# Decode attention with a GLU beside it: more filler matmuls near the end, one copy on one engine, one product in another PSUM bank

## The chip, the cores and the metric

One core of a Trainium2 chip runs the kernel. The metric is the device time of one launch in microseconds. "TensorE" does the matmuls (PE in the profile, its weight loads PEld), "VectorE" is DVE, "ScalarE" ACT, "GpSimd" POOL, and "SyncE" (SP) issues the DMAs.

## The reference

One decode step of a parallel block for two sequences (B = 2), everything in float32: a layer norm, then attention over the last 2048 positions of a cache with 32 heads of 128, and beside it a bilinear GLU.

```python
W = min(4096, max(256, Sk // 4))                      # 2048 of 8192 positions
q = (xn @ wq).reshape(B, 1, 32, 128)                  # xn = layernorm(x), D = 512
scores = einsum("bhqd,bhkd->bhqk", q, k_cache[:, :, Sk - W:]) * 128 ** -0.5
o = einsum("bhqk,bhkd->bhqd", softmax(scores), v_cache[:, :, Sk - W:])
out = x + o.reshape(B, 1, 4096) @ wo + ((xn @ w_gate) * (xn @ w_up)) @ w_down   # F = 1376
```

## The kernel before

The caches and all weights, some 159 MB, are laid out beforehand as one stream in the order of their use, and SyncE loads it piece by piece into three `step` buffers of 54 KB a partition. `blocks` writes that order out by hand; `pump` issues the next piece when all fields of an old one have been used (`done`). At the end of the order stand: V of head 29 with its rows of `wo` and the first half of V of head 31 (one piece); V of head 30; the second half of V of head 31; the `wo` rows of head 31 and three blocks of `w_down`; and then the rest of `w_down` in ever smaller pieces.

For each head the work runs through all engines. VectorE multiplies K by q, broadcast over the positions (`products`), and sums over each 128 columns (`sums`). `maxima` takes the maximum on VectorE and across partitions on GpSimd. `weights` makes the softmax weights on ScalarE: a small scaling nm, then one exponential for each sequence, which also gives the sums; GpSimd adds those across partitions. TensorE then does the product with V: `weigh` issues 16 matmuls of 512 columns into one PSUM bank (`o_ps`, two banks in turn), and `copy_out` has ScalarE copy that bank to a small tile `o_sb`. `transpose` picks the wanted columns out of it and turns them, four matmuls (eight in the trace) with `pick` as the moving operand into a few columns of the bank `tr`, and ScalarE scales them with the reciprocal of the softmax sum into `oT`. `project_o` multiplies by `wo` and adds into the accumulator bank `acc`.

Instructions stay on each engine in the order in which they are written (`InOrder`), so the order in the source is each engine's queue. Most heads go through a loop; the last ones, from line 498 on, are written out by hand, since the stream ends there and other engines' waits come into the open. `HF` is head 28. From it on `accumulate` adds in another layout: four groups of 128 columns on four parts of the bank, so that the result is spread over more partitions; for the change of layout, the sum so far is copied by VectorE to `acc_sb` and added back by TensorE ("the carried sum", line 517).

`keep_busy(n)` (line 327) is a matmul of n columns of which nobody uses the result. It writes a spare PSUM bank; it stands where TensorE would wait. `GC` is 512 and `P` is 128. Head 31 is done in two halves, as its V comes in two pieces: `last_half(0)` and `last_half(1)`, into a bank of their own, `o_ps2`. Line 539 and on copy this bank to two tiles `o_last`, one half on ScalarE and one on VectorE. Both last heads' transposes go to the bank `tr`, to different columns. `down` and `down_half` add the last of the GLU.

Every record of the trace has line 102 (the helper `InOrder`), so instructions are told apart by their tiles: `o_ps<-step,p` is the product with V, `q<-step,p` that of head 31 (its bank comes from the pool of q), `q<-xnb,mean_w` a filler, `tr<-first,o_sb` a transposition, `acc<-step,oT` a projection.

Of the kernel before, what the change touches and what calls it, by code (L numbers as in the profile page):

```python
# [8 lines left out]
F32 = mybir.dt.float32  # L9
# [7 lines left out]
P = 128  # L17
B, D, H, DH, SK, F = 2, 512, 32, 128, 8192, 1376
# [13 lines left out]
GC = HG * DH  # L32
# [85 lines left out]
def kernel(  # L118
# [7 lines left out]
    pe, dve, act, sp = (InOrder(tc, e) for e in (nc.tensor, nc.vector, nc.scalar, nc.sync))  # L126
# [3 lines left out]
    const = ctx.enter_context(tc.tile_pool(name="const", bufs=1))  # L130
    steps = ctx.enter_context(tc.tile_pool(name="steps", bufs=BUFS))
    small = ctx.enter_context(tc.tile_pool(name="small", bufs=6))
# [40 lines left out]
    def done(kind, i):  # L173
        nonlocal held
        _, key = got.pop((kind, i))
        left[key] -= 1
        if left[key] == 0 and key[0] != "f":
            del tiles[key]
            held -= 1
            pump()  # L180
# [3 lines left out]
    pick = got["pick", 0][0].rearrange("p (r s b) -> p r s b", s=2, b=B)  # L184
# [14 lines left out]
    o_ps = [ps_c.tile([P, 4 * DH], F32, name=f"o_ps{i}") for i in range(2)]  # L199
# [13 lines left out]
    tr = ps_c.tile([P, 4 * P], F32, name="tr")  # L213
# [26 lines left out]
    def side(h):  # L240

        return int(h % 3 == 0)
# [75 lines left out]
    def accumulate(lhsT, rhs, last=False):  # L318
        nonlocal n_acc
        for g in range(4):  # L320
            pe.matmul(
                acc_g[32 * g : 32 * g + M, :], lhsT, rhs[:, g * P : (g + 1) * P],
                start=(n_acc == 0), stop=last,
            )
        n_acc += 1

    def keep_busy(n):
        pe.matmul(spare[:, 0:n], mean_w, spare_in[:, 0:n], start=True, stop=True)

    def weigh(h, v, parts, first, last, into=None):  # L330

        into = o_ps[bank] if into is None else into
        for n, part in enumerate(parts):
            b, i = divmod(part, JG)
            pe.matmul(
                into[32 * i : 32 * i + 8 * B, :], p_t[h][:, b, i, :],
                v[:, FB * n : FB * (n + 1)], start=first and b == 0, stop=last and b == B - 1,
            )

    def copy_out():  # L340
        nonlocal bank
        o_sb = small.tile([P, 4 * DH], F32, name="o_sb", bufs=2)
        act.copy(o_sb, o_ps[bank])
        bank = 1 - bank
        return o_sb

    def transpose(heads, *parts):
        blk = [t[:, i : i + DH] for t in parts for i in range(0, t.shape[1], DH)]
        d = tr[:, 8 + 4 * bank : 12 + 4 * bank]
        s0, s1 = side(heads[0]), side(heads[-1]) + 1  # L350
        dst = d.rearrange("p (s b) -> p s b", b=B)[:, s0:s1, :]
        for r in range(4):
            pe.matmul(
                dst, blk[r], pick[:, r, s0:s1, :],
                start=(r == 0), stop=(r == 3),
            )
        for h in heads:
            rec = rec_t.pop(h)
            oT[h] = oT_ring[h % 4]
            for b in range(B):  # L360
                c = B * side(h) + b
                act.activation(
                    oT[h][:, b : b + 1], d[:, c : c + 1], AF.Copy,
                    scale=rec[:, b : b + 1],
                )

    def project_o(h):
        wo = got["wo", h][0]
        if h < HF:
            pe.matmul(acc, oT.pop(h), wo, start=(h == 0), stop=False)  # L370
        else:
            accumulate(oT.pop(h), wo)
        done("wo", h)

    def pv(heads):
        for h in heads:
            weigh(h, got["v", h][0], range(CK // FB), h == heads[0], h == heads[-1])
            done("v", h)
        return copy_out()

    def values(heads, busy=((), ())):
        o_sb = pv(heads)
        for n in busy[0]:
            keep_busy(n)
        transpose(heads, o_sb)
        for n in busy[1]:
            keep_busy(n)
        for h in heads:
            project_o(h)
# [110 lines left out]
    spare, o_ps2 = spare_t[:, 0, :], spare_t[:, 1, :]  # L500
# [8 lines left out]
    o_sb = pv([HF])  # L509
# [3 lines left out]
    dve.tensor_copy(acc_sb, acc)  # L513
    sums(h + 1)
    transpose([HF], o_sb)
    keep_busy(256)
    accumulate(carry, acc_sb)
    project_o(HF)
    weights(h)
# [1 line left out]
    def last_half(b):  # L521
        weigh(H - 1, got["vh", b][0], range(b * JG, (b + 1) * JG), b == 0, b == B - 1, o_ps2)
        done("vh", b)

    o_sb = pv([H - 3])
    keep_busy(320)
    maxima(h + 1)
    reciprocals(h)
    weights(h + 1)
    transpose([H - 3], o_sb)  # L530
    keep_busy(P)
    last_half(0)
# [1 line left out]
    reciprocals(h + 1)  # L534
    keep_busy(256)
    o_sb = pv([H - 2])
    keep_busy(320)
    last_half(1)
    o_last = [const.tile([P, 2 * DH], F32, name=f"o_last{i}") for i in range(2)]
    act.copy(o_last[0], o_ps2[:, : 2 * DH])  # L540
    dve.tensor_copy(o_last[1], o_ps2[:, 2 * DH :])
    transpose([H - 2], o_sb)
    bank = 1 - bank
    transpose([H - 1], *o_last)
    project_o(H - 2)
    down(2)
    project_o(H - 1)
# [103 lines left out]
```

## Time and profile before

| what | value |
|---|---|
| median of 3 runs | 384.2 us (381.69 to 384.62) |
| the profiled execution: time | 379.88 us |
| the profiled execution: span | 378.0 us, 2889 instructions |
| granted TensorE clock, mean | 0.801 |
| bytes read from HBM | 159.50 MB, 422 GB/s over the span |
| busy: PE, DVE, ACT, POOL | 257.9, 295.4, 58.8, 25.3 us |
| DMA share of the chain that ended last | 61% |

The profile is that of one execution. Its span runs from the first to the last instruction of the program; the time of the execution is 1.9 us longer. A line of the timeline or of the groups has the start or the busy time, the engine, the operation, output<-inputs with partitions and columns, the count, and in brackets for how long the engine was idle before and what released it. A matmul in float32 stands twice in the trace. The granted clock is the share of full speed that TensorE was given.

### The profile page before, as it was taken

What the parts mean: (1) busy time and instruction counts of PE and PEld (TensorE: products, weight loads), DVE (VectorE), ACT (ScalarE), POOL (GpSimd) and SP (SyncE); (2) the same over time, 40 slices, a digit from 0 to 9 for tenths busy, and PEclk for the clock granted to TensorE, in tenths of its full rate; (3) what the DMA queues carried; (4) which work ended last, traced back from release to release, by engine and by line L of the source; (5) the groups of instructions that cost most, each with busy time, mean ns of one, the idle gap of its engine ahead of it and who ended that gap; (6) DMA issues with size and microseconds to landing.
All of it is one profiled execution on the core that took longest, in us unless ns stands there. A gap on an engine that the chain in (4) does not pass through costs nothing.

```text
span 378.0 us, 2889 instructions
## 1 busy us (share of the span) xinstructions
PE 257.9 (68%) x1102; PEld 87.9 (23%) x1102; DVE 295.4 (78%) x147; ACT 58.8 (16%) x261; POOL 25.3 (7%) x74
## 2 busy tenths in 40 slices
PE   3486587988548586763858667385665868629896
PEld 3241123232112221221312112121211222203234
DVE  4299691997699499779949968994994999699930
ACT  1021002122011120201112021020202012112111
POOL 1001000010000000000000000000000001000000
PEclk9996988889897666988757698785969678557989
DMA  8999999999999999999999999999999999999993
GB/s 339 446 433 447 434 408 462 433 415 441 440 415 451 433 427 441 415 445 445 421 434 441 427 439 439 411 451 427 427 451 429 421 446 433 431 423 413 423 426 116
DMA packets 4506, 159.73 MB, mean 423 GB/s; under 512 B 501, under 2 KB 757, under 8 KB 1166
## 3 DMA queue, kind: packets, MB, share of 16 engines
q1 hardware_dynamic: 4494, 159.57, 97.9%
q8 instruction: 8, 0.13, 0.1%
q14 instruction: 4, 0.03, 0.0%
HBM read 159.50 MB, written 0.07 MB: 422 GB/s over the span
## 4 chain that ended last, share of the span: by engine, by line
DMA 61%; PE 18%; DVE 17%; ACT 2%; issue 1%; SPq 0%; DVEq 0%
DMA step<-in_stream_dram 61%; DVE step L102 8%; DVE s L102 8%; PE o_ps L102 6%; PE q L102 5%; PE acc L102 4%; PE tr L102 3%; ACT o_sb L102 1%; ACT oT L102 1%; SPq L102 0%; ACT hT L102 0%; DVE o_sb L102 0%; DVE m L102 0%; ACT hX L102 0%; DVE o_out L102 0%
## 5 line engine op out<-in xcount | busy, mean ns | idle before, releaser
L102 DVE TENSOR_TENSOR step<-step,q 128x4096 f32<-128x4096 f32 x31 | 136.6, 4407 | 53.2 <-DMA step<-in_stream_dram 53.2
L102 PE MATMUL q<-step,xnb 128*128 128x512 f32 (+1 forms) x128 | 93.3, 879 | 74.0 <-DMA step<-in_stream_dram 74.0
L102 DVE TENSOR_REDUCE s<-step 128x32 f32<-128x4096 f32 x32 | 141.4, 4419 | 1.1
L102 PE MATMUL o_ps<-step,p 128*16 128x512 f32 x496 | 69.3, 697 | 11.5 <-DMA step<-in_stream_dram 11.4
L102 PEld LDWEIGHTS q<-step,xnb 128*128 128x128 f32 x128 | 32.4, 275 | 128.4 <-DMA step<-in_stream_dram 74.6
L102 PE MATMUL acc<-step,oT 128*2 128x512 f32 (+1 forms) x88 | 34.6, 547 | 9.0 <-ACT oT L102 9.0
L102 PE MATMUL tr<-first,o_sb 128*128 128x2 f32 (+4 forms) x192 | 26.8, 258 | 15.8 <-ACT o_sb L102 12.8
L102 ACT COPY o_sb<-o_ps 128x512 f32<-128x512 f32 x23 | 13.5, 586 | 149.7 <-PE o_ps L102 149.7
L102 PEld LDWEIGHTS tr<-first,o_sb 128*128 128x128 f32 (+2 forms) x192 | 24.6, 197 | 37.5 <-ACT o_sb L102 31.3
L296 POOL PARTITION_ALL_REDUCE mm<-m x32 | 11.4, 356 | 283.6 <-DVE rec L102 178.6
L102 PEld LDWEIGHTS o_ps<-step,p 128*16 128x16 f32 x496 | 13.0, 106 | 72.2 <-issue 54.5
L102 ACT ACTIVATE nm<-mm 128x2 f32<-128x2 f32 x32 | 6.5, 204 | 125.0 <-POOL mm L296 125.0
L102 ACT ACTIVATE p<-s,nm 128x16 f32<-128x16 f32 x64 | 19.2, 300 | 1.0
L102 ACT ACTIVATE oT<-tr,rec 128x1 f32<-128x1 f32 x64 | 12.2, 260 | 27.8 <-PE tr L102 27.8
L312 POOL PARTITION_ALL_REDUCE sum<-rs x32 | 12.8, 401 | 55.3 <-ACT p L102 55.3
L102 PE MATMUL o_ps<-step,xn 128*2 128x512 f32 (+1 forms) x48 | 12.6, 579 | 0.0
L102 ACT ACTIVATION_READ_ACCUMULATOR p<-s,nm 128x1 f32 x64 | 12.0, 187 | 0.0
L102 DVE TENSOR_TENSOR step<-step,tr 128x4096 f32<-128x4096 f32 x1 | 4.4, 4420 | 9.5 <-DMA step<-in_stream_dram 9.5
L102 PEld LDWEIGHTS acc<-step,oT 128*2 128x2 f32 x88 | 3.8, 83 | 18.5 <-ACT oT L102 14.4
L102 PE MATMUL q<-xnb,mean_w 128*128 128x512 f32 (+3 forms) x18 | 7.9, 530 | 0.0
L102 PE MATMUL acc<-step,hT 128*2 128x128 f32 (+2 forms) x72 | 7.0, 308 | 0.0
L102 DVE RECIPROCAL rec<-sum 128x2 f32<-128x2 f32 x32 | 5.0, 155 | 2.3 <-POOL sum L312 2.3
(47 smaller groups left out, 44.6 us busy)
## 6 DMA issues: line engine op xcount, KB each, us to landing
step<-in_stream_dram SPq DMA_DIRECT2D x16, 6912.0 KB, 33.7
step<-in_stream_dram SPq DMA_DIRECT2D x2, 6656.0 KB, 37.2
step<-in_stream_dram SPq DMA_DIRECT2D x2, 6400.0 KB, 32.7
step<-in_stream_dram SPq DMA_DIRECT2D x1, 5376.0 KB, 15.4
step<-in_stream_dram SPq DMA_DIRECT2D x1, 4864.0 KB, 29.9
step<-in_stream_dram SPq DMA_DIRECT2D x1, 3328.0 KB, 17.0
step<-in_stream_dram SPq DMA_DIRECT2D x1, 2304.0 KB, 22.1
step<-in_stream_dram SPq DMA_DIRECT2D x2, 1024.0 KB, 16.3
```

The lines of the kernel that those rows point to most:

```text
L102: made = call(*args, **kwargs)
L296: nc.gpsimd.partition_all_reduce(mm, m, P, bass_isa.ReduceOp.max)
L312: nc.gpsimd.partition_all_reduce(sum_t[h], rs, P, bass_isa.ReduceOp.add)
```

## The change

Four edits, all in the hand-written end:

- The filler ahead of the carried sum has 512 columns and not 256.
- Two fillers, of 512 and 256 columns, are new ahead of head 29's product with V. The one ahead of the second half of head 31 has 256 columns and not 320.
- The copy of `o_ps2` is one copy of 512 columns on ScalarE into a tile of the pool of `o_sb`. The two `o_last` tiles in the permanent pool (1 KB a partition each) are gone.
- `transpose` takes one tile and, if wanted, a place for its output: head 31's goes to the first columns of the `o_ps` bank that is free then, and no longer to `tr`.

```diff
-    def transpose(heads, *parts):
-        blk = [t[:, i : i + DH] for t in parts for i in range(0, t.shape[1], DH)]
-        d = tr[:, 8 + 4 * bank : 12 + 4 * bank]
+    def transpose(heads, o_sb, into=None):
+        d = tr[:, 8 + 4 * bank : 12 + 4 * bank] if into is None else into
...
             pe.matmul(
-                dst, blk[r], pick[:, r, s0:s1, :],
+                dst, o_sb[:, r * DH : (r + 1) * DH], pick[:, r, s0:s1, :],
                 start=(r == 0), stop=(r == 3),
...
     transpose([HF], o_sb)
-    keep_busy(256)
+    keep_busy(GC)
     accumulate(carry, acc_sb)
     project_o(HF)
     weights(h)
...
+    for n in (GC, 256):
+        keep_busy(n)
     o_sb = pv([H - 3])
     keep_busy(320)
...
     o_sb = pv([H - 2])
-    keep_busy(320)
+    keep_busy(256)
     last_half(1)
-    o_last = [const.tile([P, 2 * DH], F32, name=f"o_last{i}") for i in range(2)]
-    act.copy(o_last[0], o_ps2[:, : 2 * DH])
-    dve.tensor_copy(o_last[1], o_ps2[:, 2 * DH :])
+    o_last = small.tile([P, 4 * DH], F32, name="o_sb", bufs=2)
+    act.copy(o_last, o_ps2)
     transpose([H - 2], o_sb)
-    bank = 1 - bank
-    transpose([H - 1], *o_last)
+    transpose([H - 1], o_last, o_ps[bank][:, : 2 * B])
     project_o(H - 2)
```

## The prediction

> **What bounds the kernel now.** I read first the page (where does the time go over the whole span), then the chain of waits at its end, then the timeline of the last 20 us by engine, and last the windows, for the clock. The page:
>
> ```profile
> span 378.0 us, 2889 instructions
> GB/s 339 446 433 447 434 408 462 433 415 441 440 415 451 433 427 441 415 445 445 421 434 441 427 439 439 411 451 427 427 451 429 421 446 433 431 423 413 423 426 116
> DMA 61%; PE 18%; DVE 17%; ACT 2%; issue 1%; SPq 0%; DVEq 0%
> ```
>
> The stream of caches and weights runs at some 430 GB/s in every slice but the first and the last. No edit touches it, so nothing before about 356 us moves. What can be won lies behind the stream, in the last slice and a half. The last pieces of the stream (issue on SP's queue in the timeline; below it, from the DMA view of the same moment, KB and us to landing):
>
> ```profile
> 343.44 0.43 SPq L102 DMA_DIRECT2D step<-in_stream_dram  x1
> step<-in_stream_dram SPq DMA_DIRECT2D x1, 2304.0 KB, 22.1
> 352.72 0.33 SPq L102 DMA_DIRECT2D step<-in_stream_dram  x1
> step<-in_stream_dram SPq DMA_DIRECT2D x1, 1024.0 KB, 15.3
> 354.51 0.43 SPq L102 DMA_DIRECT2D step<-in_stream_dram  x1
> step<-in_stream_dram SPq DMA_DIRECT2D x1, 128.0 KB, 17.8
> ```
>
> So head 30's V lands at 343.44 + 22.1 = 365.5, the second half of head 31's V at 352.72 + 15.3 = 368.0, and the very last piece at 354.51 + 17.8 = 372.3. The chain of waits says what happens from head 29's V on:
>
> ```profile
> 343.06 16.98 DMA step<-in_stream_dram
> ...
> 373.41 1.91 PE acc L102 x80
> ```
>
> Head 29's V lands at 360.04; from there to 375.32 the chain is TensorE nearly alone, and the last matmul is 3 us behind the last byte. The tail is bound by TensorE, not by the stream. The windows show TensorE's busy time in its first column, and the granted clock third from the end:
>
> ```profile
> 327.00:330.40 3.40, 2.69 (x13) 1.07 (x6) 3.37 (x2) 0.59 (x1) 0.00 (x0) 0.50 0.94 407
> 330.40:333.80 3.40, 2.67 (x6) 0.80 (x6) 3.40 (x1) 0.41 (x2) 0.00 (x0) 0.50 0.90 392
> ...
> 354.30:357.70 3.40, 3.04 (x14) 1.36 (x12) 3.40 (x2) 1.31 (x7) 0.00 (x0) 1.00 0.96 415
> 357.70:361.10 3.40, 1.74 (x28) 0.58 (x32) 3.40 (x2) 0.36 (x3) 0.40 (x1) 1.00 0.95 408
> 361.10:364.50 3.40, 3.40 (x18) 1.38 (x6) 1.34 (x3) 1.38 (x6) 0.48 (x2) 0.50 0.99 425
> 364.50:367.90 3.40, 3.40 (x34) 1.68 (x37) 0.17 (x1) 0.41 (x2) 0.28 (x1) 1.00 0.98 412
> ```
>
> A stretch of 3.4 us with 3.04 us of matmul is followed by one at full clock; one with 1.74 us is followed by one at half; that one is full of work, and the clock is back. So the tail loses its clock from 361.1 to 364.5, right where TensorE is the chain. The timeline, by engine (start, us, what, and in brackets the idle time before):
>
> ```profile
> 352.21 1.91 PE L102 MATMUL o_ps<-step,p 128*16 128x512 f32 x16
> 355.74 0.97 PEld L102 LDWEIGHTS tr<-first,o_sb 128*128 128x128 f32 x8 [0.86 <-issue]
> 356.63 0.30 PEld L102 LDWEIGHTS q<-xnb,mean_w 128*128 128x128 f32 x2
> 357.91 0.40 PE L102 MATMUL acc<-acc_sb,first 2*2 2x128 f32 x8 [0.57 <-DVE acc_sb L102]
> 358.23 0.40 PE L102 MATMUL acc<-step,oT 128*2 128x128 f32 x8
> 360.09 2.67 PE L102 MATMUL o_ps<-step,p 128*16 128x512 f32 x16 [1.46 <-DMA step<-in_stream_dram]
> 362.56 0.36 POOL L296 PARTITION_ALL_REDUCE mm<-m  x1 [3.94 <-DVE rec L102]
> 362.80 0.59 ACT L102 COPY o_sb<-o_ps 128x512 f32<-128x512 f32 x1 [4.74 <-PE o_ps L102]
> 363.28 0.21 ACT L102 ACTIVATE nm<-mm 128x2 f32<-128x2 f32 x1
> 363.82 0.29 ACT L102 ACTIVATE p<-s,nm 128x16 f32<-128x16 f32 x1
> 365.02 0.47 PE L102 MATMUL q<-xnb,mean_w 128*128 128x128 f32 x2
> 365.42 1.05 PE L102 MATMUL q<-step,p 128*16 128x512 f32 x8
> 366.62 0.70 PE L102 MATMUL q<-xnb,mean_w 128*128 128x256 f32 x2
> 367.25 1.91 PE L102 MATMUL o_ps<-step,p 128*16 128x512 f32 x16
> 369.09 0.81 PE L102 MATMUL q<-xnb,mean_w 128*128 128x320 f32 x2
> 369.82 1.05 PE L102 MATMUL q<-step,p 128*16 128x512 f32 x8
> 370.81 1.05 PE L102 MATMUL tr<-first,o_sb 128*128 128x2 f32 x8
> 370.94 0.37 ACT L102 COPY o_last<-q 128x256 f32<-128x256 f32 x1 [1.13 <-PE q L102]
> 371.35 0.42 DVE L102 COPY o_last<-q 128x256 f32<-128x256 f32 x1 [6.37 <-ACT o_last L102]
> 371.89 0.41 ACT L102 ACTIVATE oT<-tr,rec 128x1 f32<-128x1 f32 x2 [0.58 <-PE tr L102]
> 372.36 0.27 PE L102 MATMUL tr<-first,o_last 128*128 128x2 f32 x1 [0.50 <-ACT oT L102]
> 373.34 0.40 PE L102 MATMUL acc<-step,oT 128*2 128x128 f32 x8
> ```
>
> Here `q<-xnb,mean_w` is a filler (`keep_busy`), `q<-step,p` is half of head 31's PV. Two holes of TensorE, 0.57 and 1.46 us, stand ahead of head 29's PV: those are what emptied the 357.70 window.
>
> **The change part by part.** Fillers ahead of head 29's PV: what they cost. A filler of 256 columns holds TensorE from 366.62 to 367.25, 0.63 us; one of 320 from 369.09 to 369.82, 0.73. That is 1.6 ns a column and 0.2 us once. So 512 and 256 in a row cost 0.2 + 768 x 1.6 ns = 1.45 us at full clock: from 358.6, where head 28's projection ends (358.23 + 0.40), to 360.05. Head 29's V starts to be used at 360.09, so they fit into the wait, with nothing to spare; cost 0, and if the cover is gone (TensorE late, or at half clock) up to 1.4 us. The longer filler ahead of the carried sum (256 to 512 columns, 0.4 us) fits into the hole of 0.57 before 357.91, which VectorE's copy of the sum ends: 0, and 0.4 without cover.
>
> What they bring: the window from 357.70 gets 1.4 us more, 3.1 us of work, as much as the 354.30 window that kept the clock. Then at full clock, on the path: head 29's PV takes 1.91 as at 352.21 and not 2.67, so it ends at 362.00; ScalarE's copy starts 0.06 later and takes 0.59: 362.65; head 29's eight transposes start 0.04 on and hold TensorE 0.89 (355.74 to 356.63, with 0.03 for the last): 363.61; the filler of 128 takes 0.40 (365.02 to 365.42): 364.01. There the first half of head 31's PV starts, which started at 365.42: -1.41. The next thing that could be late is head 31's weights. VectorE's sums do not move; GpSimd's maximum is there at 362.92; in the trace ScalarE's nm-to-second-exponential took from 363.28 to 364.11, 0.83, so it is done at some 363.0 + 0.83 = 363.83, 0.2 ahead of its use. Were ScalarE no earlier than now, 364.11 plus a release would cost 0.15 of the 1.41. Bounds of this part: -1.41 and, if the clock is not held, 0.
>
> What closes the clock decides here. In the rows it fell behind a window whose longest hole was 1.46 us. [...] I take the rows.
>
> The filler ahead of head 31's second half, 320 to 256: -0.10. The waits for the stream behind it: head 30's PV goes from 367.25 to 364.01 + 1.83 = 365.84, landing 365.5; head 31's second half to 365.84 + 1.84 + 0.63 = 368.31, landing 368.0. Both still come after their data, by 0.3 us; a stream that is 0.5 us later would take 0.2 back from each.
>
> The last copy whole on ScalarE, and another bank. Today ScalarE copies one half of o_ps2, VectorE starts on the other only when ScalarE has done (371.35, released by o_last), then head 31's transposes wait 0.50 more until ScalarE has read head 30's columns of the same bank. From the start of head 30's transposes to that of head 31's: 370.81 to 372.36, 1.55. After it: the whole copy is 0.59 like any 128x512 copy here, starts 0.12 after head 30's transposes (369.31 + 0.12), and is done at 370.02; those transposes hold TensorE 0.92, to 370.23; the copy is done 0.2 earlier, and head 31's picks go to a bank that ScalarE does not read then. So 1.55 becomes 0.92: -0.63. Queued behind the copy on ScalarE are head 30's two scalings, which need the transposes' end (369.31 + 1.05 = 370.36) anyway: no new wait. VectorE loses its half and had nothing behind it but the output copy. Bounds: -0.63, and 0 if head 31's transposes still waited until ScalarE has read head 30's columns (370.36 + 0.06 + 0.41 + 0.06 = 370.89, again 1.58 behind head 30's).
>
> The rest, 373.34 to 375.32, is 80 matmuls that move as a block. Shifted by 2.1 they end at 373.2; the last piece lands at 372.3 and is needed only by the last few, and the 1024 KB ahead of the last 768, at 430 GB/s 2.4 us behind the 368.0, by matmuls at 371.4: no wait. The stream is thus the limit of any gain here, at 375.3 - 372.5 = 2.8 us.
>
> A side effect: the two o_last tiles leave the permanent pool, 2 KB a partition, and the step tiles after it move down by 2 KB. The three step tiles lie 54 KB apart, so neighbours already differ by an odd multiple of 2 KB and the GB/s row shows no pattern of it: 0. The trace before can't exclude a shift; I bound it by 1% of the stream's 372 us, 3.7 us either way.
>
> **Sum**: -1.41 - 0.10 - 0.63 = -2.1 us. The profiled execution took 379.88 us (span 378.0): 377.7 after it. The three runs shown had 381.69 to 384.62, median 384.2, so 4.3 us above the profiled one; the tail is the same program, so I take 384.2 - 2.1 = 382.1.
>
> **Rivals.** *The fillers overrun* (the other side). The clock opens again only after a full window: 2.69 us of work at half clock (327.00) left the next at half. Where the windows fall otherwise around 340, TensorE does heads 26 and 27 at half clock up to one window longer, 1.7 us of work late. The first 0.6 disappears in the hole before 357.91, but with the longer filler only 0.15. From the point where TensorE comes to the fillers 0.7 us late, head 29's PV starts more than that behind its V; at the worst 1.25 us. There the wait was small already, the old kernel kept its clock too, and only the -0.73 of the two later edits stands against it: +0.5, 384.7. For: nothing ties these windows to the kernel's start. Against: in this trace TensorE was on time.
>
> *The fillers bring nothing*, because the clock drops all the same or would not have dropped: only -0.73 is left, 383.5. For: the opening and closing are known from a few windows. Against: 3.04 kept it.
>
> *Another rule of the clock.* If only an idle stretch as long as a whole window closed it, the 1.46 us hole would not be the cause, and filling it would change nothing: again 383.5. For: one drop in one trace is little. Against: it is the drop at 361.1, with nothing longer before it than the brackets show. [...]
>
> *The stream's rate moves with the 2 KB shift*: 382.1 with 3.7 off or on, 378.4 or 385.8. For: nothing in this trace has the tiles there. Against: the flat GB/s row.
>
> **How the numbers follow.** Forecast 0.50; overrun 0.20; fillers bring nothing 0.13; the other rule 0.05; the shift 0.12. A measurement of this kernel can tell about 1%, 3.8 us; the 2.1 is 0.55%. Since the three times alone lie 2.9 us apart, three in ten of the forecast's cases (0.15) may come out beyond 1%, with 0.06 from the shift and 0.01 from the rest: faster 0.22. Slower: 0.06 of the shift, 0.06 of overrun and spread, 0.12. Same: 0.66. Range: 381.69 - 2.1 = 379.6 below, 384.7 + 0.5 = 385.2 above, which leaves out most of the shift and little else. The forecast's own range is that of the runs shifted by the sum, 379.6 to 382.5.
>
> **What would show it.** Right: the stretch 361.10 to 364.50 at clock 1.00; head 29's PV at 1.9 us; head 31's first half at 364.0; its transposes straight behind head 30's, waiting for nobody; the last matmul 0.9 us behind the last piece. Wrong: head 29's PV behind a filler after its V has landed; the clock at 0.50 in the tail; head 31's first half waiting for p; the tail waiting for a piece of the stream; the pieces landing at another pace. Then the step named is the one that failed.

## The result, and the profile after

The kernel after took 378.06 us (median of 6 runs, 377.73 to 378.46), the kernel before in the same comparison 382.45 (6 runs, 380.04 to 384.62): a ratio of 0.9883, 95% interval 0.9841 to 0.9925, 4.4 us. The forecast was 382.1 with a range from 379.6: the forecast gain of 2.1 is right in sign and half of the 4.4, and the time lies outside the range. Later comparisons, with more runs of before, gave less: over 101 further runs of before on four chips the median is 380.56 (379.50 to 385.05), over 21 runs of the kernel after (6 here, 7 in E2, there with the old addresses, 8 in E17) it is 378.1 (377.62 to 378.94). By these the change is worth 2.5 us, 0.65%; the other 1.9 of the 4.4 is how much longer these six runs of before were than the later ones.

The page of the kernel after, and the issue and landing (KB, us) of the last piece of its stream:

```profile
span 376.3 us, 2896 instructions
DMA 62%; PE 21%; DVE 15%; ACT 1%; issue 1%; SPq 0%; DVEq 0%
354.56 0.43 SPq L102 DMA_DIRECT2D step<-in_stream_dram  x1
step<-in_stream_dram SPq DMA_DIRECT2D x1, 128.0 KB, 17.8
```

The stream ends at 372.4 (354.56 + 17.8), as before. The windows of its tail (TensorE's busy time first, the granted clock third from the end):

```profile
356.00:359.40 3.40, 3.40 (x29) 1.70 (x28) 3.40 (x3) 1.20 (x7) 0.40 (x1) 1.00 0.95 410
359.50:362.90 3.40, 3.40 (x22) 1.04 (x20) 2.98 (x3) 0.40 (x1) 0.29 (x1) 1.00 1.01 434
362.90:366.30 3.40, 3.40 (x33) 1.86 (x34) 0.17 (x1) 1.41 (x8) 0.46 (x2) 1.00 0.97 411
366.30:369.70 3.40, 3.40 (x27) 0.77 (x26) 0.00 (x0) 0.58 (x1) 0.00 (x0) 1.00 0.99 411
369.70:373.10 3.40, 3.40 (x83) 3.31 (x83) 0.00 (x0) 1.41 (x5) 0.00 (x0) 1.00 0.51 194
```

In this tail no hole is left and the clock does not fall. TensorE's timeline in the same trace:

```profile
359.03 1.56 PE L102 MATMUL q<-xnb,mean_w 128*128 128x512 f32 x4
360.52 1.91 PE L102 MATMUL o_ps<-step,p 128*16 128x512 f32 x16
...
364.45 1.05 PE L102 MATMUL q<-step,p 128*16 128x512 f32 x8
...
370.64 1.03 PE L102 MATMUL o_ps<-first,o_sb 128*128 128x2 f32 x8
```

The x16 of a product with V is eight matmuls in the kernel, each twice in the trace. TensorE came 0.4 us late to the fillers here, so head 29's PV starts 0.5 behind its V, and what follows is 0.4 late against the forecast. The second trace of the same kernel (E17) has TensorE on time:

```profile
span 375.8 us, 2896 instructions
358.51 1.56 PE L102 MATMUL q<-xnb,mean_w 128*128 128x512 f32 x4
360.03 1.91 PE L102 MATMUL o_ps<-step,p 128*16 128x512 f32 x16
363.95 1.05 PE L102 MATMUL q<-step,p 128*16 128x512 f32 x8
365.79 1.91 PE L102 MATMUL o_ps<-step,p 128*16 128x512 f32 x16
368.25 1.05 PE L102 MATMUL q<-step,p 128*16 128x512 f32 x8
370.15 1.03 PE L102 MATMUL o_ps<-first,o_sb 128*128 128x2 f32 x8
371.11 0.40 PE L102 MATMUL acc<-step,oT 128*2 128x128 f32 x8
```

Forecast for these rows, from the PV at 360 on, were 360.05, 364.01, 365.84, 368.31, 370.23 and 371.2, and 375.9 for the span (the last two are the old 373.34 and 378.0 less 2.1): each within 0.1 us. The question was therefore not the tail of the kernel after, but what the kernel before does in the runs that were not traced.

### The profile page after: what moved, and what is told of

It reads as the page before. It is cut to its first block, busy times and chain, and to the rows that moved or that the text cites. A ratio compares the mean times of both kernels' runs of the same rounds, so it can differ in the third digit from the quotient of the medians.

```text
span 376.3 us, 2896 instructions
## 1 busy us (share of the span) xinstructions
PE 259.8 (69%) x1106; PEld 88.1 (23%) x1106; DVE 295.1 (78%) x146; ACT 59.0 (16%) x261; POOL 25.2 (7%) x74
## 4 chain that ended last, share of the span: by engine, by line
DMA 62%; PE 21%; DVE 15%; ACT 1%; issue 1%; SPq 0%; DVEq 0%
DMA step<-in_stream_dram 62%; PE o_ps L102 8%; DVE s L102 7%; DVE step L102 7%; PE q L102 6%; PE acc L102 4%; PE tr L102 3%; ACT o_sb L102 0%; SPq L102 0%; ACT oT L102 0%; DVE o_sb L102 0%; ACT hT L102 0%; DVE m L102 0%; ACT hX L102 0%; DVE o_out L102 0%
## 5 line engine op out<-in xcount | busy, mean ns | idle before, releaser
L102 PEld LDWEIGHTS tr<-first,o_sb 128*128 128x128 f32 (+2 forms) x192 | 23.7, 192 | 37.6 <-ACT o_sb L102 32.8
L102 PE MATMUL q<-xnb,mean_w 128*128 128x512 f32 (+3 forms) x22 | 9.1, 511 | 0.0
```

The lines of the kernel that those rows point to most:

```text
L102: made = call(*args, **kwargs)
```

## The experiments

Theory A: the gain is the clock and the waits of the last 16 us. Theory B: the stream's pace depends on where the step tiles lie, which the change moves by 2 KB. All times are medians; the runs of before beside them are those of the same chip.

**E1, the addresses alone**, and **E2, the kernel after with the old addresses.**

```diff
 E1, against before
-    o_last = [const.tile([P, 2 * DH], F32, name=f"o_last{i}") for i in range(2)]
+    o_whole = small.tile([P, 4 * DH], F32, name="o_sb", bufs=2)
+    o_last = [o_whole[:, : 2 * DH], o_whole[:, 2 * DH :]]
 E2, against after
+    const.tile([P, 4 * DH], F32, name="hold")
     o_out = const.tile([P, P], F32, name="o_out")
```

> The kernel before with nothing but the addresses of the one after: the two o_last halves are views of one tile of the o_sb pool, so that the permanent pool is 2 KB shorter and the step tiles lie 2 KB lower; copies, fillers and banks as before. Theory A (the time came from the clock and the waits of the last 16 us): no change, a ratio of 1.000 +- 0.004, and the same spread of some 4 us as the kernel before. Theory B (the stream's pace depends on where the step tiles lie, and the time before varies with it): most of the 4.4 us, a ratio of 0.990 or less, with a spread below 1 us.

> The kernel after with an unused tile of 2 KB in the permanent pool, so that the step tiles lie where they did before. Theory A: 378.1 us like the kernel after, ratio 0.988, spread below 1 us. Theory B: two fifths to half of the gain at most, 380 to 382 us, with the spread of before.

E1: 380.90 (379.84 to 385.53, 12 runs), before 380.54; ratio 1.0005 (0.9973 to 1.0037). E2: 377.95 (377.69 to 378.41); 0.9929 (0.9901 to 0.9957). Theory B falls on both: the addresses are worth nothing that these runs show, and the kernel after keeps its time and its narrow spread without them.

**E3, the filler edits alone**, and **E4, the whole copy and the other bank alone** (addresses held as in E2).

```diff
 E3, against before
-    keep_busy(256)          # ahead of the carried sum
+    keep_busy(GC)
...
+    for n in (GC, 256):
+        keep_busy(n)
     o_sb = pv([H - 3])
...
-    keep_busy(320)          # ahead of last_half(1)
+    keep_busy(256)
 E4, against before
-    o_last = [const.tile([P, 2 * DH], F32, name=f"o_last{i}") for i in range(2)]
-    act.copy(o_last[0], o_ps2[:, : 2 * DH])
-    dve.tensor_copy(o_last[1], o_ps2[:, 2 * DH :])
+    o_last = small.tile([P, 4 * DH], F32, name="o_sb", bufs=2)
+    act.copy(o_last, o_ps2)
...
-    bank = 1 - bank
-    transpose([H - 1], *o_last)
+    transpose([H - 1], o_last, o_ps[bank][:, : 2 * B])
```

> The kernel before with the three filler edits alone; copies, tiles and bank as before. Theory A: the larger part of the gain and the narrow spread: 378.8 us, 0.7 above the kernel after, and in the trace the clock at 1.00 from 357 to the end. Theory B: at most the 1.4 us of the clock, with the spread of before. If the variation of before comes from the last copies, the spread stays here too.

> The kernel before with the whole copy on ScalarE and head 31's transposes in the other bank, the addresses held as before by an unused tile; fillers as before. Theory A: -0.6 us, a ratio of 0.998, the spread of before, and the clock at 0.50 for one stretch in the tail. Theory B: the same. If the copies or the shared bank are what makes the kernel before vary, then this one is narrow and gains 3 us.

E3: 379.74 (378.17 to 380.34, 12 runs), before 380.54; ratio 0.9967 (0.9946 to 0.9988). E4: 379.25 (377.69 to 383.58); 0.9950 (0.9923 to 0.9977). Alone, the fillers bring 0.8 us and not 1.5, copy and bank 1.3 and not 0.6; both at once, in E2, bring 2.6. The runs of each fall into groups: E3 has 3 at 378.2 to 378.5 and 9 at 379.5 to 380.3, and none above; E4 has 4 at 377.7 to 378.1, 7 at 379.0 to 379.6 and one at 383.6. E3 was expected narrow at 378.8, and 9 runs of 12 are above that; E4 was expected at a ratio of 0.998, which lies outside its interval. The two traces are one of E3's short group (378.35) and one of E4's middle group (379.55); their chains have, E3 first:

```profile
371.90 1.91 PE acc L102 x80
360.45 2.71 PE o_ps L102 x16
373.12 1.91 PE acc L102 x80
```

In E3's, head 29's PV takes 1.87 us and the last 80 matmuls 1.91, as at full clock. In E4's, head 29's PV takes 2.71 us and not 1.91 and the filler behind it 1.36 and not 0.74, while the transposes from 364.53 on (0.99) and the last 80 matmuls (1.91) have their length at full clock again. Each of the two edits leaves open the place that the other one closes, and in E4's trace the time was lost there.

**E8, the old bank in the kernel after.**

```diff
-    transpose([H - 1], o_last, o_ps[bank][:, : 2 * B])
+    bank = 1 - bank
+    transpose([H - 1], o_last)
```

> The kernel after, with head 31's transposes in the old bank beside head 30's, as before; the whole copy on ScalarE and all fillers stay. Theory A: head 31's transposes wait until ScalarE has read head 30's columns, 0.6 us, and in the runs in which a window of the clock closes around that hole the last 80 matmuls go at half clock, 1.6 us more: 378.6 to 380.3, median 379.5, so the bank is the whole gain of that edit and the whole copy alone brings nothing. Rival (the wait in the kernel before was for the two copies in series): 378.0 to 378.2.

379.71 (378.35 to 380.45, 12 runs), before 380.65; ratio 0.9968 (0.9946 to 0.9989). That is E3's time (379.74): with the fillers in and the bank shared, the whole copy on ScalarE brings nothing measurable. The other bank was not run with the two copies left as they were, so that it needs nothing of the copy is not shown. Windows and a line of the timeline:

```profile
369.70:373.00 3.30, 2.80 (x52) 2.67 (x56) 0.00 (x0) 1.41 (x5) 0.00 (x0) 1.00 0.49 187
373.10:374.90 1.80, 1.75 (x52) 1.32 (x40) 0.00 (x1) 0.00 (x0) 0.00 (x0) 0.50 0.00 0
371.11 1.05 PE L102 MATMUL tr<-first,o_sb 128*128 128x2 f32 x8 [0.50 <-ACT oT L102]
```

The wait for ScalarE's reading of head 30's columns is back with 0.50 us, and behind a stretch with that one hole the clock falls and most of the last matmuls go at half (80 take 2.71 us, and 1.91 in the kernel after).

**B1 to B3, three more traces of the kernel before.**

> The kernel before, unchanged, for another trace of it. Theory A2: its time follows from the clock alone: about 380 us with one stretch of 3.4 us at half clock behind 357, 381.5 to 382 with a second drop that takes the last matmuls, 384 with half clock for two windows or more in a row; the last piece of the stream lands at 372.3 +- 0.3 in each. Rival: in a slow trace the last piece lands later by as much as the time is longer.

> As the look before: the kernel before, unchanged. Theory A2: the time goes with the number of half-clock stretches behind 357 us, the stream's end stays at 372.3 +- 0.3. Rival: the stream's end moves with the time.

> As the two looks before: the kernel before, unchanged. Theory A2: the time goes with the number of half-clock stretches behind 357 us, the stream's end stays at 372.3 +- 0.3. Rival: the stream's end moves with the time.

379.84, 380.41 and 379.53 us; the last piece of the stream lands between 372.2 and 372.4 in all three, as expected. The windows of B2, and the last 80 matmuls in the chains of B1, B2 and B3, in this order:

```profile
357.70:361.10 3.40, 1.82 (x28) 0.57 (x32) 3.40 (x2) 0.27 (x2) 0.40 (x1) 1.00 0.92 393
361.10:364.50 3.40, 3.40 (x28) 1.73 (x24) 1.36 (x4) 1.81 (x8) 0.75 (x2) 1.00 0.99 423
364.50:367.90 3.40, 3.40 (x35) 1.06 (x24) 0.06 (x1) 0.17 (x1) 0.00 (x0) 1.00 0.98 414
368.00:371.30 3.30, 2.80 (x22) 1.53 (x20) 0.42 (x1) 1.10 (x4) 0.00 (x0) 1.00 0.91 360
371.40:374.80 3.40, 3.40 (x57) 2.59 (x60) 0.00 (x0) 0.41 (x2) 0.00 (x0) 0.50 0.05 17
372.07 3.25 PE acc L102 x80
372.32 3.57 PE acc L102 x80
371.97 3.00 PE acc L102 x80
```

In none of the three does the clock fall at 361, where the prediction's trace had it; in all three it falls behind 371, and the last 80 matmuls take 3.0 to 3.6 us and not 1.9. The two kinds cost alike, so the time says nothing of which it was. B2 also shows that busy time, as the profile counts it, is not what the clock goes by: 1.82 us busy of 3.4 kept it, 2.80 of 3.3 lost it. The second stretch holds head 30's transposes and the first of head 31's, each of which moves 2 columns only. In the prediction's trace of before, the stretch with the same hole, and the same busy time, lies 3.4 us later and kept the clock to the last matmul; it holds 65 matmuls and not 22:

```profile
371.40:374.70 3.30, 2.80 (x65) 2.65 (x68) 0.37 (x1) 0.83 (x4) 0.00 (x0) 1.00 0.05 16
```

None of the three is one of the runs above 381, of which before has 38 in 101.

**E5, before without the four fillers behind head 29's PV.**

```diff
     o_sb = pv([H - 3])
-    keep_busy(320)
...
-    keep_busy(P)
...
-    keep_busy(256)
     o_sb = pv([H - 2])
-    keep_busy(320)
```

> The kernel before without its four fillers behind head 29's PV (320, 128, 256 and 320 columns). Theory A2 (the runs of before at 384 us are those in which the clock stays at half for two or three windows of 3.4 us, since the tail at half clock has too little streaming work to open it): TensorE has up to 1.5 us less to do, and yet the kernel gets slower, 382 to 385 us, with the clock at 0.50 for most of 361 to 375 in the trace. Rival (those runs have another cause, the stream or the start, and a filler is only work): 379.0 to 380, as much faster as the fillers' uncovered part, with the same few runs at 384.

379.97 (377.94 to 382.72, 12 runs), before 380.65; ratio 0.9967 (0.9935 to 0.9999). Not slower: the expectation missed. Five of its runs (377.94 to 378.23) are as short as the kernel after, which suggests that fillers of this kind are work like any other where the clock holds. The trace (380.54 us) has the three stretches at half clock that the theory wanted, but not the time of 382 to 385:

```profile
355.70:359.00 3.30, 2.83 (x28) 1.40 (x26) 3.30 (x3) 1.20 (x7) 0.30 (x1) 1.00 0.96 413
359.10:362.40 3.30, 2.31 (x12) 0.49 (x16) 3.27 (x3) 0.00 (x0) 0.00 (x0) 0.50 1.01 436
362.50:365.80 3.30, 2.60 (x15) 1.40 (x7) 0.05 (x2) 1.38 (x6) 0.75 (x2) 0.50 0.95 403
365.90:369.20 3.30, 3.30 (x26) 1.09 (x30) 0.04 (x1) 0.41 (x2) 0.00 (x0) 0.50 0.99 417
```

**E10, before without the filler ahead of the carried sum, with two more traces of the same kernel (E10b, E10c)**, to make a drop near 359 us more frequent and to catch a run at 384.

```diff
     transpose([HF], o_sb)
-    keep_busy(256)
     accumulate(carry, acc_sb)
```

> The kernel before without its filler of 256 columns ahead of the carried sum; it lies in a wait, so no work is taken off the path. Theory A3 (the runs at 384 are those in which a clock window ends near 359, just behind that filler, finds too little streaming in it, and the tail then stays at half for three windows): with 0.4 us less streaming there, windows that end anywhere from about 357.5 to 360 drop the clock: far more runs at 383 to 385, a quarter to a half of them, median 381 to 384. Rival (they have another cause): 380.5 with one run in ten at 384.

> The same kernel for another trace. Theory A3: if its time is 383 or more, the clock falls between 357.5 and 360 and is at 0.50 for two windows or more, with the stream's last piece at 372.3 as ever; if it is about 380, the clock falls in the last stretch alone.

> The same kernel for another trace, with the same expectation: 383 or more goes with half clock from before 360 on, about 380 with a drop in the last stretch alone.

E10: 381.10 (380.62 to 384.69, 12 runs), before 380.51; ratio 1.0014 (0.9990 to 1.0037); only one of the 12 runs is above 383, not a quarter. E10c took 381.51; E10b took 384.21, and that is a trace of the kind that was wanted. Its windows, its chain, and issue and landing of the stream's last piece:

```profile
355.90:359.20 3.30, 2.21 (x26) 1.18 (x24) 3.30 (x3) 1.20 (x7) 0.38 (x1) 1.00 0.95 409
359.30:362.60 3.30, 2.52 (x12) 0.49 (x16) 3.14 (x3) 0.00 (x0) 0.03 (x1) 0.50 1.01 436
362.70:366.00 3.30, 3.30 (x17) 1.93 (x9) 0.17 (x1) 1.38 (x6) 0.62 (x2) 0.50 0.96 407
366.10:369.50 3.40, 3.40 (x22) 1.36 (x21) 0.00 (x0) 0.41 (x2) 0.00 (x0) 0.50 0.99 418
369.50:372.90 3.40, 3.40 (x24) 1.02 (x28) 0.00 (x0) 0.58 (x1) 0.00 (x0) 1.00 0.52 197
373.00:376.30 3.30, 2.80 (x32) 2.07 (x28) 0.42 (x1) 0.82 (x4) 0.00 (x0) 1.00 0.00 0
376.40:379.70 3.30, 3.24 (x80) 2.50 (x68) 0.01 (x1) 0.28 (x2) 0.00 (x0) 0.50 0.00 0
360.08 3.61 PE o_ps L102 x16
...
365.06 1.50 PE tr L102 x8
...
376.23 3.44 PE acc L102 x80
354.51 0.43 SPq L102 DMA_DIRECT2D step<-in_stream_dram  x1
step<-in_stream_dram SPq DMA_DIRECT2D x1, 128.0 KB, 17.8
```

The clock falls at 359.3, stays at half for three stretches of 3.4 us, opens, and falls a second time in front of the last 80 matmuls. The stream ends at 372.3, as ever. So a run at 384 needs no slower stream: the tail alone makes it. E5's trace has the same three stretches at half, without the four fillers and without the second fall: its last 80 matmuls start 2.16 us earlier (374.07 against 376.23) and take 1.91 us and not 3.44. These two differences are the 3.7 us between the two times.

The other two traces of this kernel, E10 (381.13) and E10c, lie between. By their chains head 29's PV takes 3.61 and 3.62 us, as in E10b, the transposes behind it, from 365.03 and 365.33 on, 0.79 and not 1.50, and the last 80 matmuls, from 374.07 and 374.38 on, 2.54 and 2.61 and not 1.91. The clock is thus down before head 29's PV, back at 365 or so, and falls again within the last 80. E10c's chain:

```profile
360.45 3.62 PE o_ps L102 x16
```

So all three traces of E10 have the early fall that the expectation wanted, but it costs 381 where the clock is back at 365 or so and 384 only where it stays at half to 369.5. E10c's own expectation, 383 or 380, fits neither its time nor its clock.

**E6, one filler in place of two; E7, three; E11, the shorter one ahead of the carried sum** (all against after).

```diff
 E6
-    for n in (GC, 256):
-        keep_busy(n)
+    keep_busy(GC)
 E7
-    for n in (GC, 256):
+    for n in (GC, GC, 256):
 E11
     transpose([HF], o_sb)
-    keep_busy(GC)
+    keep_busy(256)
```

> The kernel after with the filler of 512 columns alone ahead of head 29's PV, without that of 256. In the trace of the kernel after TensorE came 0.45 us late to head 29's V. Theory A: where TensorE comes late, 0.4 us faster, 377.6 us, and where it is on time the hole of 0.4 us is too short to drop the clock: median 377.7 to 378.0, narrow. Rival (the margin of the clock is thin): some runs at 379 and above, median above 378.2.

> The kernel after with one more filler of 512 columns ahead of head 29's PV, 0.85 us of work at full clock. If the wait for head 29's V has no cover left, as the trace of the kernel after says: all of it on the path, 378.9 us, and nothing of it lost again in waits. If there is cover left: 378.0 to 378.4.

> The kernel after with the filler ahead of the carried sum back at 256 columns. Theory A3: TensorE is some 0.4 us earlier where it came late, so most runs are at 377.6 to 377.9; but a window that ends near 359 has less streaming in it, so one run in ten or so is above 380. Rival (the longer filler is only work): 377.6 to 377.9 in all runs.

E6: 377.73 (377.61 to 378.19, 6 runs); ratio to before 0.9915 (0.9882 to 0.9947). E7: 378.56 (378.34 to 379.27, 12 runs); 0.9930 (0.9906 to 0.9954). E11: 377.78 (377.44 to 378.13, 6 runs); 0.9921 (0.9891 to 0.9952). E7's three fillers and head 29's PV behind them:

```profile
358.64 2.42 PE L102 MATMUL q<-xnb,mean_w 128*128 128x512 f32 x6
360.99 1.48 PE L102 MATMUL o_ps<-step,p 128*16 128x512 f32 x12
```

PV starts 1 us later than in E17, where it found its V just landed, and the median is 0.5 us above that of the 21 runs of after: beyond the landing, a filler is on the path. In the two traces nothing of it is made up behind: the last 80 matmuls start at 372.14 in E7 (chain) and at 371.11 in E17 (timeline). That the medians differ by 0.5 only is not explained; in the other trace of the kernel after, TensorE itself came late. The fillers of the kernel after are longer than needed; with one of 512 columns the clock is kept in the trace (head 29's PV 1.84 us, the last 80 matmuls 1.91) and no run is above 378.19; with the shorter one ahead of the carried sum none is above 378.13, and the median is 0.3 us below that of the 21 runs. Rare runs above 380, which E11 was to bring out, six runs cannot exclude.

**E9, E6 also without the filler of 128 columns behind head 29's transposes; E9b, again beside the kernel after, unchanged (E17).**

```diff
     transpose([H - 3], o_sb)
-    keep_busy(P)
```

> The kernel with one filler of 512 ahead of head 29's PV, and without the filler of 128 columns behind head 29's transposes. Theory A: TensorE is the chain from 360 to the end, so the filler's 0.4 us comes off: 377.3 us, since head 30's V then still lands 0.1 us before its use, and the clock holds: spread below 0.8 us. Rival (the filler keeps the clock): some runs at 379 and above.

> The kernel after, unchanged, beside the version with fewer fillers on one chip. Theory A: 378.0 us, all runs within 0.5 of it, 2.5 below the median of before. If the gain of the first comparison (4.4 us) is the kernel's own and not that of the six runs of before, 376 to 377 or before at 382.

> The kernel after with one filler of 512 ahead of head 29's PV, and without that of 128 behind head 29's transposes, again. Theory A: 377.5 us, 0.5 below the kernel after on the same chip, since both fillers were work on TensorE's path; no run above 378.5. Rival: the difference of the earlier runs was that of two chips' draws: 378.0.

E9: 377.49 (377.22 to 377.82); ratio to before 0.9914 (0.9884 to 0.9944). On one chip: E17 378.24 (377.62 to 378.94, 8 runs), 0.9923 (0.9898 to 0.9949); E9b 377.47 (377.39 to 377.62, 6 runs), 0.9906 (0.9872 to 0.9940); before 381.34 (13 runs, 380.01 to 385.05). With two fillers fewer the kernel is 0.8 us below the kernel after, and none of its six runs is above the fastest of the eight of E17. This version beats both.

## Why the prediction was wrong in its base, and what of its parts held

**The base failed.** "The tail is the same program, so I take 384.2 - 2.1" is the step that broke. It took the 4.3 us between the three runs and the profiled one for something that a shift of the tail leaves alone and that the kernel after would have too. It has not: its 21 runs end at 378.94. Two things were wrong in it. The larger is the base itself. Two of the three runs were above 384, while of the 101 later runs 9 are at 383 or more; with the median of these, 380.56 - 2.1 = 378.5, and 378.1 was measured. Three of the first six runs were at 383 or more, which at 9 in 101 would happen about once in a hundred times, so luck of the draw is a poor explanation, and what else was different in that comparison stays open. The other is the place of the spread. E10b shows that runs at 384 can be made in the tail itself, by the clock, with the stream's end unmoved; the kernel after has none in 21 runs, where before had 9 of 101 at 383 or more and 38 at 381 or more. What the change takes away is therefore also the spread, and a sum read from one trace belongs to the time of that trace: 379.88 - 2.1 = 377.7, against 378.1 measured. The lower end of the range, 381.69 - 2.1, has the same fault. No trace caught the kernel before itself at 384; that its runs there are like E10b's is argued from the one missing filler between the two.

**The sum came out, two of its terms were not what was thought, and that is partly luck.** In the traced pair the time went from 379.88 to 378.11, and with TensorE on time the span came to 375.8, forecast 375.9. For a trace whose clock falls at 361 the terms are right, row by row. But the -1.41 for the fillers is what they bring where the clock falls at 361, in one of the four traces of before; in the three others it fell behind 371. Over the runs the fillers bring 0.8, copy and bank 1.3 (E3, E4): one term too large, the other too small by about as much. The -0.63 of the bank was its wait alone: the step missed that the same hole of 0.50 us, between the transposes of heads 30 and 31, can let the clock fall for the last 80 matmuls, 1.1 to 1.7 us more (B1 to B3 against the 1.91 of the prediction's trace and of E3, which have the hole too and keep the clock).

**What closes the clock was read from the wrong column.** "A stretch of 3.4 us with 3.04 us of matmul is followed by one at full clock; one with 1.74 us is followed by one at half" was one pair in one trace; B2 keeps it with 1.82 and loses it with 2.80. The stretch of 2.80 us spends a good part of its time on transposes of 2 columns, and that of 1.82 on matmuls of 128 and 512. That the clock goes by the columns streamed is the author's estimate from these stretches; no run varied it alone. The margin is thin: 1.74 us lost the clock in the one trace and 1.82 kept it in the other, with the same matmuls in both. The length of a stretch can be read from the whole trace, in steps of 0.1 us: the 24 stretches at half clock of before last some 3.4, 6.8, 10.2 or 23.9 us, the 26 of after some 3.4, 6.8, 10.2 or 13.7, which is to within the step one, two, three, four or seven times 3.41; those of E10b, 359.3 to 369.5, are three times 3.4. Where the stretches begin is not the same from run to run: before opened its clock at 344.1 and after, on a grid shifted by 1.8 us, at 345.9, and the kernel before lost its clock at 361.1 in one run and at 371.4 in another (B2).

**The rivals.** The overrun is real in mechanism (after: 0.5 us late; E7: 1 us) but small beside what it protects. Its premise that the clock opens only after a full stretch holds roughly: in the trace of before it opened behind stretches with 3.07 us of matmul or more of 3.41 and stayed at half behind those with 2.71 or less, but in that of after it opened behind one with 2.58 and stayed at half behind one with 2.84. "The fillers bring nothing" is refuted by E3 and by the missing runs at 381 and more. The rule that only an idle stretch as long as a whole window closes the clock is refuted once more: 0.50 us is the longest hole of E8's stretch ahead of its fall. The 2 KB shift brings nothing that E1 or E2 shows. The bank's wait was as the prediction had it, and the copy in series was not its cause: E8, with the one copy, has the same 0.50, and in the other bank no wait is left ahead of head 31's transposes (after: from 370.64, 0.91 behind head 30's; E8: 1.55).

## What to carry to other kernels

A time and a profile are two different executions: where they lie 1% apart, ask first which part of the kernel could vary, and whether the change removes that part, before adding a difference from the one to the other. Ahead of a tail that one engine sets, a hole of 0.50 us cost 0.6 to 1.7 us more in the traces in which the clock fell behind it (2.54 us in E10, 3.57 in B2 for the last 80 matmuls, against 1.91), so a change should be priced at every place where the clock could fall and not at the one where it fell in the trace at hand. Here a filler was worth its columns only up to the moment at which the data landed (E7: PV 1 us later, the median 0.5 us higher); with two fillers fewer no run was above 377.82 (E9, E9b), and the median was 0.8 us below that of the kernel after on the same chip (E9b, E17).

## What was not expected of the hardware

The same program loses the clock at different places from run to run (at 361.1 in the prediction's trace, behind 371 in B1 to B3), with times from 379.5 to 385.1 us over 101 runs. At half clock a stretch can be 3.30 of 3.30 us busy (E10b, 362.70) and be followed by half clock again, while one 3.40 of 3.40 us busy was followed by full clock (before, 361.10). The transposes of 2 columns, which fill a good part of the former at half clock (1.50 us for eight in the chain of E10b), seem to count for little; no run tested this.
